# Two early loads moved from SyncE's queue to ScalarE's, in a fused linear-attention and cosine-gated MLP kernel

## The chip, the cores and the metric

The kernel runs on one core of a Trainium2 chip. A core has TensorE (PE: matrix products, written to PSUM), VectorE (DVE), ScalarE (ACT: functions such as exp, ln, sin), GpSimd (POOL) and SyncE (SP, which here issues DMA transfers), each with its own instruction stream, tied together by semaphores. The metric is device time in microseconds for one execution of the whole program.

## The reference

For each of 4 x 8 heads, a state of 48 x 48 is decayed and added to at each of 768 tokens; the result for all heads goes through a two-layer MLP with the gate h * cos(h).

```python
f = 1.0 / (1.0 + np.exp(-f_logit))
for t in range(S):                       # S = 768, D = 48
    state = f[:, :, t, :, None] * state + np.einsum('bhd,bhe->bhde', k[:, :, t], v[:, :, t])
    y[:, :, t] = np.einsum('bhd,bhde->bhe', q[:, :, t], state)
x = y.transpose(0, 2, 1, 3).reshape(3072, 384)
h = x @ w_in                             # 384 x 2048
out = (h * np.cos(h)) @ w_out            # 2048 x 384
```

q, k, v and f_logit are float32 of shape (4, 8, 768, 48), the output is float32 of shape (3072, 384).

## The kernel before, in words

The recurrence is computed in chunks. A chunk has 128 tokens; the work unit of the first half is a pair of chunks (256 tokens, all 8 heads), and there are 12 pairs, three for each batch entry. A pair n needs its parts of f, k, q and v, of shape 128 partitions x 8 heads x 2 tokens x 48. For the pairs 0 and 1 (`HALVES`) f, k and q are loaded and processed in two halves of four heads each, named `.0` and `.1`: `f0.1` is the second half of f for pair 0. Each half is 192 KB.

The steps for one half u of pair n, in the order in which they depend on each other:

- `f`, `q`, `k`: the three loads (line 299, function `load`).
- `ex`, `ln` (ACT, lines 332 and 336): exp(-f_logit), then ln(1 + ...), which gives the negative log of the gate.
- `fx` (ACT, line 350): the gate of the odd tokens, exp of the negative logarithm. It needs `ln`.
- `cum` (PE, lines 377 and 383): running sums of the logarithms, by a product with a triangular matrix.
- `eb`, `ei` (ACT, line 394 for the pairs in halves): the decay factors exp(-sum) and exp(+sum).
- `qa` (DVE, line 341) and `ka` (line 354): q and k of one token of each two are multiplied in place; `qa` needs f after `ex` and the loaded q, `ka` needs `fx` and the loaded k.
- `qm`, `km` (line 407): q and k times their decay factors, as bf16.
- `tq`, `tk` (PE, line 437), `qkt` (line 200): transposes and their copy out of PSUM.
- `sc`, `am` (lines 459 and 465 or 471), `ps`, `st`, `sz` (lines 489, 507, 513), `y`, `yi`, `xe` (line 541 and 200): scores, state and output of the pair.

The MLP takes the 3072 tokens in units of 128 or 256: `h` (line 608, first product), `co` (line 613, sine with a quarter turn), `g` (line 580, gate), `o` (line 630, second product), `ot` and `out`.

Nothing is planned at run time or by a scheduler: the string `ORDER` lists every step as `name:engine and buffers`, with the letters T (PE), S (ACT), V (DVE), G (POOL) and Y (SP). `emit` walks this list and emits each step's instructions on the engine that the letter names, so each engine's program is the list cut to its letter. The words that count here are, in the order of the list, with other engines left out:

```
SP before:   f0.1 f0.0 q0.0 k0.1 f1.1 k0.0 q0.1 q1.1 f1.0 k1.1 v0 q1.0 k1.0 f2 v1 w0.0 ...
ACT before:  (table load) ex0.1 ln0.1 ex0.0 ln0.0 fx0.0 eb0.0 ei0.0 eb0.1 ei0.1 fx0.1 ex1.1 ln1.1 fx1.1 ...
DVE before:  (constants, zeros) qa0.0 qm0.0 ka0.1 km0.1 ka0.0 km0.0 qa0.1 qa1.1 qm0.1 zvt.0 qm1.1 qkt0.1 ...
```

All loads are on SP's queue. In each engine's program an instruction waits for what it needs and holds back what stands behind it. In gaps of the beginning PE multiplies zeros (`zf0` to `zf46`, line 267, results never read).

[...] Steps that need exp or ln carry `table="E"`, the sine `table="S"`. `emit` starts with `table = None`, so the first step with "E", `ex0.1`, is preceded by a table load (line 673); line 673 also gives the loads at later changes from "S" to "E".

Of the kernel before, what the change touches and what calls it, by code (L numbers as in the profile page):

```python
# [15 lines left out]
B, H, S, D = 4, 8, 768, 48  # L16
# [20 lines left out]


ORDER = """
zsp.1:V zqk.1:V zqk.2:V zsz.0:G f0.1:Y0 ex0.1:S ln0.1:S1 f0.0:Y ex0.0:S ln0.0:S fx0.0:S zf0:T6  # L40
zf1:T6 zf2:T6 zf3:T6 zf4:T6 zf5:T6 zf6:T6 zf7:T6 cum0.1:T0 zf8:T6 cum0.0:T1 zsz.3:V eb0.0:S0
q0.0:Y0 ei0.0:S0 eb0.1:S ei0.1:S fx0.1:S qa0.0:V k0.1:Y0 qm0.0:V2 ka0.1:V zqk.0:G f1.1:Y1 km0.1:V
ex1.1:S zf9:T6 zf10:T6 zf11:T6 zf12:T6 zf13:T6 zf14:T6 zf15:T6 tq0.0:T2 ln1.1:S1 zf16:T6 zf17:T6
zf18:T6 zf19:T6 zf20:T6 tk0.1:T3 cum1.1:T0 k0.0:Y ka0.0:V km0.0:V zf21:T6 tk0.0:T fx1.1:S q0.1:Y
qa0.1:V q1.1:Y1 qa1.1:V ei1.1:S1 eb1.1:S1 qm0.1:V zvt.0:V qm1.1:V0 qkt0.0:S0 zf22:T6 zf23:T6 zf24:T6
# [146 lines left out]
def describe(nc, cpool, ppool, q, k, v, f_logit, moe_w_in, moe_w_out, out):  # L192
    G = Graph()
    eng = lambda e: {"DVE": nc.vector, "POOL": nc.gpsimd, "ACT": nc.scalar, "SP": nc.sync}[e]
# [63 lines left out]
    tiles = [ppool.tile([128, 1024], F32, name=f"ps_{i}") for i in range(4)]  # L258
# [37 lines left out]

    def load(name, val, src, b, c, h0, h1):
        tok = src[b, h0:h1, 2 * C * c:2 * C * c + 2 * C, :] if nc is not None else None
        G.step(name, ("SP",), lambda e: eng(e).dma_start(  # L299
            out=val.ap.rearrange("p h e d -> p h (e d)"),  # L300
            in_=tok.rearrange("h (p e) d -> p h (e d)", e=2)), writes=[val])

    def fetch(kind, pool, src, n, b, c, cut):

        whole = Val(pool)
        hs = [whole.part(lambda a, u=u: a[:, 4 * u:4 * u + 4]) for u in range(2)]
        if cut:
            for u in range(2):
                load(f"{kind}{n}.{u}", hs[u], src, b, c, 4 * u, 4 * u + 4)
        else:  # L310
            load(f"{kind}{n}", whole, src, b, c, 0, H)
        return whole, hs
# [343 lines left out]
def emit(tc, G, tiles):  # L656
    nc = tc.nc
    plan = []
    for word in ORDER.split():
        name, how = word.split(":")  # L660
        plan.append((G.steps[name], LETTER[how[0]], [int(x) for x in how[1:].split(",") if x]))
    assert len(plan) == len(G.steps)
    table, users = None, [[] for _ in tiles]
    for s, e, places in plan:
        for w in s.writes:
            v = w.whole
            if v.pool is not None and v.slot is None:
                v.slot = places.pop(0)
            w.first, w.final = not w.begun, w.left == 1
            w.begun, w.left = True, w.left - 1  # L670
        if s.table is not None:
            if s.table == "E" and table != "E":
                nc.scalar.preload_act_table_set("natural_log_exp_and_others")
            table = s.table
        n0 = nc.next_id()
        s.fn(e)
        made = (nc.find_inst_by_name(f"I-{i}") for i in range(n0 + 1, nc.next_id()))
        apart(tc, users, s, e, [i for i in made if i is not None])


def apart(tc, users, s, e, made):


    vals = [v.whole for v in s.reads + s.writes]
    banks = {b for v in vals if isinstance(v.pool, Banks) for b in range(v.slot, v.slot + v.pool.size)}
    home = lambda v: v.whole.pool is not None and not isinstance(v.whole.pool, Banks)
    uses = [(v, v.whole, i) for i, vs in enumerate((s.reads, s.writes)) for v in vs if home(v)]

    def meet(theirs):
        for v, w, wr in uses:  # L690
            for v2, w2, wr2 in theirs:
                if (wr or wr2) and w.pool is w2.pool and w.slot == w2.slot:
                    if w is not w2 or v is v2 or v is w or v2 is w2:
                        return True
        return False
    for t in {b // 2 for b in banks}:
        for engine, others, theirs, there in users[t]:
            if engine != e and not banks & theirs and not meet(there):
                for b in others:
                    for a in made:  # L700
                        tc.declare_no_dep(a, b, reason="the steps use different PSUM banks")
        users[t].append((e, made, banks, uses))
        del users[t][:-WITHIN]


@with_exitstack
def kernel(
    ctx: ExitStack,
    tc: tile.TileContext,
    q: bass.AP,  # L710
    k: bass.AP,
    v: bass.AP,
    f_logit: bass.AP,
    moe_w_in: bass.AP,
    moe_w_out: bass.AP,
    out: bass.AP,
):
    nc = tc.nc
    cpool = ctx.enter_context(tc.tile_pool(name="const", bufs=1))
    ppool = ctx.enter_context(tc.tile_pool(name="psum", bufs=1, space=bass.MemoryType.PSUM))  # L720
    with tc.manual_schedule():
        G, tiles = describe(nc, cpool, ppool, q, k, v, f_logit, moe_w_in, moe_w_out, out)
        emit(tc, G, tiles)
# [30 lines left out]
```

## Time and profile before

| what | value |
|---|---|
| median of 3 runs | 181.56 us (181.17 to 181.99) |
| profiled execution, its own time | 181.48 us |
| its span on the core | 179.4 us |
| busy: PE, DVE, ACT, POOL | 96%, 79%, 75%, 56% of the span |
| granted TensorE clock | full |
| first load issued, first function on ACT | 0.73 us, 3.49 us |
| queue of SP | 71968 packets, 33.37 MB |
| queue of ACT | 288 packets, 0.20 MB (two stores at the end) |

The span runs from the first instruction to the last one; the execution's time has 2.08 us more. In the rows of the profile a first number is a time from the start of the span in us and the second a length; `<-DMA q` in brackets names what ended the wait ahead of an instruction, with the idle time. `SPq` and `ACTq` are the sequencers of SP and ACT, which issue DMA transfers and take up waits; a row `DMA_DIRECT2D` is the issuing of a transfer, and "to landing" is the time from that issue to the semaphore that tells of the last byte. `PE busy (x)` and the like in rows of windows are busy time and number of instructions of PE, PEld (weight loads), DVE, ACT and POOL, then the granted clock, the busy share of the 16 DMA engines, and GB/s.

### The profile page before, as it was taken

The numbers are of one execution on the slowest core, as the hardware profiler recorded it, in microseconds if no ns is written. First come the engines' busy times: TensorE is split into PE (matmuls) and PEld (weight loads), VectorE is DVE, ScalarE is ACT, GpSimd is POOL, SyncE is SP. The second block draws the span as 40 slices with busy tenths as digits, with TensorE's granted clock in tenths as the row PEclk, the third lists the DMA queues.
The fourth block names the chain that finished last, engine by engine and source line by source line (L and its number), as shares of the span: only waits on it lengthen the run. The fifth ranks groups of instructions, "written<-read, shape, count | busy, mean of one in ns | idle before, by whom it ended". The sixth has DMA issues, their size and how long they took to land.

```text
span 179.4 us, 6015 instructions
## 1 busy us (share of the span) xinstructions
PE 172.6 (96%) x2553; PEld 125.2 (70%) x2553; DVE 142.5 (79%) x221; ACT 133.7 (75%) x190; POOL 100.5 (56%) x125
## 2 busy tenths in 40 slices
PE   7999999999999899999999999999999989999993
PEld 2565589867777588865588866888666668887662
DVE  6599999997598999979698896989768858874321
ACT  5969998988999998897689995877762478754020
POOL 4046559665979899989988959996061000000000
PEclk9999999999999999999999999999999999999999
DMA  5999999999999999789989999965308102000033
GB/s 125 278 262 306 371 331 355 324 286 277 243 263 283 252 272 218 160 161 257 270 203 219 253 212 263 192 107 117 91 4 211 41 17 74 4 0 0 26 114 127
DMA packets 72282, 33.94 MB, mean 189 GB/s; under 512 B 65344, under 2 KB 70720, under 8 KB 72256
## 3 DMA queue, kind: packets, MB, share of 16 engines
q1 hardware_dynamic: 71968, 33.37, 75.3%
q8 instruction: 20, 0.33, 0.8%
q10 hardware_dynamic: 288, 0.20, 0.3%
q14 instruction: 6, 0.05, 0.1%
HBM read 25.17 MB, written 4.72 MB: 167 GB/s over the span
## 4 chain that ended last, share of the span: by engine, by line
PE 75%; DVE 12%; DMA 5%; issue 3%; SPq 2%; ACT 1%; DVEq 0%; ACTq 0%
PE ps L608 35%; PE ps L630 29%; PE ps L541 4%; DVE sz L513 3%; PE ps L459 3%; DMA q<-in_q_dram 3%; SPq L299 2%; DMA out_dram<-ot 2%; PE ps L489 2%; DVE ps L507 2%; DVE am L471 2%; DVE am L465 1%; DVE ot L200 1%; PE ps L437 1%; DVE qkt L200 1%
## 5 line engine op out<-in xcount | busy, mean ns | idle before, releaser
L630 PE MATMUL ps<-w_out_bf,g 128*128 128x384 bf16 (+1 forms) x400 | 68.8, 320 | 0.0
L580 DVE TENSOR_TENSOR g<-ps,co 128x1024 bf16<-128x1024 f32 x48 | 60.8, 1307 | 9.2 <-ACT co L613 9.1
L608 PE MATMUL ps<-x,w_in_bf 128*128 128x256 bf16 (+1 forms) x624 | 66.2, 264 | 0.3 <-DVE g L580 0.2
L608 PEld LDWEIGHTS <-w_in_bf 128*128 128x128 bf16 x624 | 56.6, 98 | 8.4 <-DVE x L200 0.3
L613 ACT ACTIVATE co<-ps,halfpi 128x1024 bf16<-128x1024 f32 x48 | 51.9, 1113 | 10.7 <-PE ps L608 10.6
L630 PEld LDWEIGHTS <-g 128*128 128x128 bf16 x400 | 36.8, 98 | 20.4
L471 DVE TENSOR_TENSOR am<-ps,pmask 128x1024 bf16<-128x1024 f32 x22 | 26.2, 1215 | 2.4 <-PE ps L459 2.2
L407 POOL TENSOR_TENSOR qk<-k,bi 128x384 bf16<-128x384 f32 x20 | 19.9, 1001 | 9.8 <-ACT bi L398 9.3
L407 POOL TENSOR_TENSOR qk<-q,b 128x384 bf16<-128x384 f32 x20 | 20.1, 1005 | 2.9 <-ACT b L398 1.2
L354 POOL TENSOR_TENSOR k<-k,f 128x384 f32<-128x384 f32 (+1 forms) x11 | 10.6, 967 | 11.9 <-DMA k<-in_k_dram 9.6
L513 DVE TENSOR_TENSOR sz<-ps,b 64x192 bf16<-64x192 f32 x40 | 14.1, 352 | 2.6 <-PE ps L489 1.6
L200 ACT COPY ot<-ps 128x384 f32<-128x384 f32 (+1 forms) x14 | 6.1, 451 | 12.7 <-PE ps L630 12.7
L267 PE MATMUL ps<-zero 128*128 128x512 bf16 x47 | 14.4, 427 | 1.2 <-DVE zero L206 1.2
L200 DVE COPY ot<-ps 128x384 f32<-128x384 f32 (+1 forms) x12 | 6.4, 534 | 11.2 <-PE ps L630 9.7
L200 POOL COPY vt<-vb 64x384 bf16<-64x384 bf16 x27 | 13.4, 502 | 2.5 <-ACT vb L200 1.3
L507 DVE TENSOR_TENSOR ps<-ps,sz 64x192 f32<-64x192 f32 x32 | 11.7, 366 | 2.5 <-PE ps L489 1.5
L332 ACT ACTIVATE f<-f 128x768 f32<-128x768 f32 (+1 forms) x14 | 10.5, 751 | 3.8 <-DMA f<-in_f_logit_dram 3.7
L200 ACT COPY vt<-vb 64x384 bf16<-64x384 bf16 x21 | 10.7, 509 | 0.4
L366 POOL TENSOR_TENSOR sp<-ls 128x384 bf16<-128x384 f32 x10 | 10.0, 999 | 1.7 <-ACT ls L336 1.4
L200 DVE CAST x<-ps 128x384 bf16<-128x384 f32 x16 | 8.5, 552 | 1.6 <-PE ps L541 1.5
L200 ACT CAST x<-ps 128x384 bf16<-128x384 f32 x8 | 3.9, 483 | 7.9 <-PE ps L541 7.9
L613 ACT ACT_TABLE_LOAD x6 | 7.7, 1283 | 2.7 <-PE ps L608 2.6
(65 smaller groups left out, 177.8 us busy)
## 6 DMA issues: line engine op xcount, KB each, us to landing
v<-in_v_dram SPq DMA_DIRECT2D x12, 384.0 KB, 5.6
out_dram<-ot SPq DMA_DIRECT2D x22, 192.0 KB, 2.9
f<-in_f_logit_dram SPq DMA_DIRECT2D x10, 384.0 KB, 5.4
q<-in_q_dram SPq DMA_DIRECT2D x10, 384.0 KB, 6.2
k<-in_k_dram SPq DMA_DIRECT2D x10, 384.0 KB, 7.0
g<-in_moe_w_in_dram SPq DMA_DIRECT2D x4, 768.0 KB, 9.0
g<-in_moe_w_out_dram SPq DMA_DIRECT2D x4, 768.0 KB, 8.4
f<-in_f_logit_dram SPq DMA_DIRECT2D x4, 192.0 KB, 3.8
```

The costliest lines, as they stand in the source:

```text
L200: (nc.scalar.copy if e == "ACT" else eng(e).tensor_copy)(out=o, in_=i)
L267: G.step(f"zf{i}", ("PE",), lambda e, dump=dump: nc.tensor.matmul(dump.ap, lhsT=zero[:, 0:128], rhs=zero, start=True, stop=True), writes=[ ...
L332: nc.scalar.activation(out=flat(t.ap), in_=flat(t.ap), func=AF.Exp, scale=-1.0)
L354: eng(e).tensor_mul(out=w.ap[:, :, 0, :], in0=w.ap[:, :, 0, :], in1=t.ap[:, :, 0, :])
L407: G.step(f"{nm}{n}.{u}", ("POOL", "DVE"), lambda e, u=u, j=j, src=src, dec=dec: eng(e).tensor_mul(out=qkp[u][j].ap[:, :, :, 0:D], in0=swap ...
L471: G.step(f"am{n}.{u}", ("DVE",), lambda e, u=u, sc=sc: nc.vector.tensor_mul(out=am[u].ap.rearrange("p r b n -> p (r b) n"), in0=sc.ap.rear ...
L507: nc.vector.tensor_add(out=view()[s], in0=view()[s], in1=S0.ap[s, :, r, :])
L513: eng(e).tensor_mul(out=new.ap[s, :, r, :].rearrange("p (u a) n -> p u a n", u=2), in0=view()[s].rearrange("p (u a) n -> p u a n", u=2), i ...
L580: nc.vector.tensor_mul(out=o.rearrange("p b (n e) -> p b e n", e=2), in0=ph.ap.rearrange("p (b e n) -> p b e n", e=2, n=64), in1=co.ap.rea ...
L608: nc.tensor.matmul(ph.ap[:, i * T:(i + 1) * T].rearrange("p (g t) -> p g t", t=C), lhsT=w_in_bf[:, kk, f0:f0 + 128], rhs=xa[:, :, kk, :], ...
L613: G.step(f"co{m}.{j}", ("ACT",), lambda e, ph=ph, co=co: nc.scalar.activation(out=co.ap, in_=ph.ap, func=AF.Sin, bias=halfpi), reads=[ph], ...
L630: nc.tensor.matmul(po.ap[:, 0:c1 - c0], lhsT=gap[:, j, i * C:(i + 1) * C], rhs=w_out_bf[:, j, c0:c1], start=(po.first and j == 4 * s), sto ...
```

## The change

The loads `q0.0` and `k0.1` go from SP to ACT. In the list they now stand right behind `f0.1` and `f0.0` and ahead of `ex0.1`, and `f0.0` stands ahead of `ex0.1` and `ln0.1`; SP's program keeps its order without the two. The function `load` names ACT as an engine that may issue, and `emit` now starts with the table set "E" loaded explicitly ahead of the whole list, so that ACT's program begins with the table load, then issues `q0.0` and `k0.1`, then goes on with `ex0.1` as before. No other step moves on any engine.

```diff
 ORDER = """
-zsp.1:V zqk.1:V zqk.2:V zsz.0:G f0.1:Y0 ex0.1:S ln0.1:S1 f0.0:Y ex0.0:S ln0.0:S fx0.0:S zf0:T6
+zsp.1:V zqk.1:V zqk.2:V zsz.0:G f0.1:Y0 f0.0:Y q0.0:S0 k0.1:S0 ex0.1:S ln0.1:S1 ex0.0:S ln0.0:S fx0.0:S zf0:T6
 zf1:T6 zf2:T6 zf3:T6 zf4:T6 zf5:T6 zf6:T6 zf7:T6 cum0.1:T0 zf8:T6 cum0.0:T1 zsz.3:V eb0.0:S0
-q0.0:Y0 ei0.0:S0 eb0.1:S ei0.1:S fx0.1:S qa0.0:V k0.1:Y0 qm0.0:V2 ka0.1:V zqk.0:G f1.1:Y1 km0.1:V
+ei0.0:S0 eb0.1:S ei0.1:S fx0.1:S qa0.0:V qm0.0:V2 ka0.1:V zqk.0:G f1.1:Y1 km0.1:V
...
     def load(name, val, src, b, c, h0, h1):
         tok = src[b, h0:h1, 2 * C * c:2 * C * c + 2 * C, :] if nc is not None else None
-        G.step(name, ("SP",), lambda e: eng(e).dma_start(
+        G.step(name, ("SP", "ACT"), lambda e: eng(e).dma_start(
             out=val.ap.rearrange("p h e d -> p h (e d)"),
             in_=tok.rearrange("h (p e) d -> p h (e d)", e=2)), writes=[val])
...
-    table, users = None, [[] for _ in tiles]
+    table, users = "E", [[] for _ in tiles]
+    nc.scalar.preload_act_table_set("natural_log_exp_and_others")
```

## The prediction, made before the changed kernel ran

> **What bounds the kernel now.** I read the page first, then the chain of waits in its first 30 us, then the order of time of ScalarE (ACT) and VectorE (DVE) in that stretch, and then when each early load lands. The page's chain, by engine:
>
> ```profile
> span 179.4 us, 6015 instructions
> PE 75%; DVE 12%; DMA 5%; issue 3%; SPq 2%; ACT 1%; DVEq 0%; ACTq 0%
> ```
>
> The profiled execution took 181.48 us, its span 179.4, so 2.08 us lie around the span. My sum is made against 181.48; the median of the three runs is 181.56, 0.08 more. TensorE holds three quarters of the chain, but not its beginning. The chain in order of time (start, length, what):
>
> ```profile
> 1.25 0.49 SPq L299
> ...
> 5.04 4.51 DMA q<-in_q_dram
> ...
> 9.68 0.36 DVE q L341
> ...
> 22.76 0.48 DVE x L200
> ...
> 23.28 6.74 PE ps L608 x83
> ```
>
> Up to 5.04 us the chain is SyncE (SP) issuing loads one after another (the row shown is its second); then one transfer, the half q1.1 of the second pair, lands at 5.04 + 4.51 = 9.55; then DVE works to 23.24, and TensorE goes on from 23.28. What is lost or won before 23.28 is handed to TensorE, so I count it to the end one for one.
>
> Read at its face, this chain says that an SP issue fewer ahead of q1.1 is time won. DVE in order of time says how much:
>
> ```profile
> 5.93 0.36 DVE L341 SCALAR_TENSOR_TENSOR q<-f,q 128x192 f32<-128x192 f32 x1 [1.29 <-DMA q<-in_q_dram]
> 6.43 0.56 DVE L407 TENSOR_TENSOR qk<-q,b 128x384 bf16<-128x384 f32 x1
> 7.34 0.36 DVE L354 TENSOR_TENSOR k<-k,f 128x192 f32<-128x192 f32 x1 [0.35 <-ACT f L350]
> 9.07 0.35 DVE L341 SCALAR_TENSOR_TENSOR q<-f,q 128x192 f32<-128x192 f32 x1
> 9.68 0.36 DVE L341 SCALAR_TENSOR_TENSOR q<-f,q 128x192 f32<-128x192 f32 x1 [0.25 <-DMA q<-in_q_dram]
> ```
>
> The wait for q1.1 is 0.25 us. Before it DVE works without a pause from 7.34 to 9.42, and it could begin at 7.34 because ACT had finished the gate fx0.1. So behind the chain shown lies a second one, only 0.25 us shorter, and it runs through ACT:
>
> ```profile
> 0.73 1.28 ACT L673 ACT_TABLE_LOAD   x1 [0.73 <-PEq L738]
> 3.49 0.52 ACT L332 ACTIVATE f<-f 128x384 f32<-128x384 f32 x1 [1.47 <-DMA f<-in_f_logit_dram]
> 4.04 0.52 ACT L336 ACTIVATE sp<-f 128x384 bf16<-128x384 f32 x1
> 4.50 0.52 ACT L332 ACTIVATE f<-f 128x384 f32<-128x384 f32 x1
> 6.93 0.38 ACT L350 ACTIVATE f<-sp 128x192 f32<-128x192 bf16 x1
> ```
>
> ACT starts when the first f half (f0.1) lands, takes ex0.0 at 4.50, and ends fx0.1 at 7.31. Now the landings: issue times in the first fence (f0.0 is the 1.25 of the chain), and time from issue to landing in the second, in the order f0.1, f0.0, q0.0, k0.1.
>
> ```profile
> 0.73 1.00 SPq L299 DMA_DIRECT2D f<-in_f_logit_dram  x2
> 1.79 0.50 SPq L299 DMA_DIRECT2D q<-in_q_dram  x1
> 2.33 0.51 SPq L299 DMA_DIRECT2D k<-in_k_dram  x1
> ```
>
> ```profile
> f<-in_f_logit_dram SPq DMA_DIRECT2D x1, 192.0 KB, 2.7
> ...
> f<-in_f_logit_dram SPq DMA_DIRECT2D x1, 192.0 KB, 3.2
> ...
> q<-in_q_dram SPq DMA_DIRECT2D x1, 192.0 KB, 4.0
> ...
> k<-in_k_dram SPq DMA_DIRECT2D x1, 192.0 KB, 4.2
> ```
>
> They land at 0.73 + 2.7 = 3.43, 1.25 + 3.2 = 4.45, 1.79 + 4.0 = 5.79 and 2.33 + 4.2 = 6.53 us. The second f half, f0.0, lands 0.05 us before ACT takes it at 4.50: it has **no slack**, and fx0.1, DVE's step at 7.34 and all after it hang on it. From the fourth landing (6.53) to the eighth (q1.1, 9.55) there are four loads in 3.02 us, 0.755 each, while SP issues one in about 0.55 (1.79 to 2.33). So the loads queue in the DMA engines and not at SP: 196.6 kB in 0.755 us is 260 GB/s.
>
> **The change, part by part.**
>
> *SP's side.* Two issues go, and all later ones on SP come about 2 x 0.54 = 1.1 us earlier (1.79 to 2.33 to 2.88 by the rows' spacing), q1.1's too. It does not land 1.1 us earlier: before it the same eight halves have to move, six through SP's queue and two through ACT's, and the eighth landing stays near 9.55. Even if it came early, DVE gains at most its 0.25 us of waiting; then fx0.1 holds it. Gain taken: 0, bounds 0 and -0.25.
>
> [...]
>
> *ACT's side.* q0.0 and k0.1 stand on ACT behind the table load and ahead of ex0.1. Two issues at about 0.5 us (SP's rows) are done by 1.8 us at the earliest start, or by 3.1 if they wait for the load's end at 2.01. ACT waits for f0.1 until 3.49 either way, so the issues cost ACT nothing; without that cover they would cost 1.0 us. The table load is the first instruction of ACT before and after, so naming it ahead of the plan costs nothing.
>
> When do they go out? Two places show ACT's sequencer ahead of its engine:
>
> ```profile
> 51.17 1.28 ACT L673 ACT_TABLE_LOAD   x1
> ```
>
> ```profile
> L398 ACTq EVENT_SEMAPHORE  x1: 1002/1002/1002, 51.7 to 51.7; - x1
> ```
>
> ```profile
> 170.93 0.92 ACT L200 COPY ot<-ps 128x384 f32<-128x384 f32 x3 [5.07 <-PE ps L630]
> 171.66 0.34 ACTq L642 DMA_DIRECT2D out_dram<-ot  x1
> ```
>
> A wait is taken up at 51.7, 0.5 us into a table load that ends at 52.45; and a DMA is issued at 171.66 while the three copies ahead of it run to 171.85. So I expect q0.0 to be issued during the first table load, some 0.1 to 0.5 us after SP's f0.1, and k0.1 about 0.5 us later.
>
> *The price.* Then q0.0 and k0.1 travel **beside f0.1 and f0.0** and no longer behind them. What the DMA engines moved (the last two columns are their busy share and GB/s):
>
> ```profile
> 1.00:2.00 1.00, 0.81 (x2) 0.28 (x3) 0.51 (x8) 1.00 (x1) 0.92 (x4) 1.00 0.07 18
> 2.00:3.00 1.00, 1.00 (x4) 0.43 (x3) 0.93 (x5) 0.02 (x1) 0.63 (x2) 1.00 0.94 224
> 3.00:4.00 1.00, 1.00 (x4) 0.33 (x3) 0.88 (x7) 0.51 (x1) 0.00 (x0) 1.00 0.93 236
> 4.00:5.00 1.00, 1.00 (x7) 0.52 (x6) 0.64 (x3) 0.97 (x3) 0.00 (x0) 1.00 0.96 227
> 5.00:6.00 1.00, 1.00 (x13) 0.52 (x12) 0.07 (x1) 0.90 (x3) 0.00 (x0) 1.00 1.13 309
> ```
>
> By these rows the engines are 0.93 to 0.96 busy, so a second stream is paid by the first. f0.1's 196.6 kB have moved at 2 + (196.6 - 18) / 224 = 2.80, and it lands at 3.43: 0.63 us from moved to landed. How late f0.0 comes, no row of before shows, since there one queue is at work; the bounds:
> - nothing, if the second queue only takes what is free;
> - three halves moved when f0.0 is through (q0.0 half served): 705 - 227 = 478 kB by 4.0, the missing 112 at 227 GB/s, so 4.49 + 0.63 = 5.12, 0.67 us late;
> - four halves, in equal shares: 705 kB by 5.0, the missing 81 at 309, so 5.26 + 0.63 = 5.89, 1.44 us late;
> - four halves, taken by the fourth landing of before: 6.53, 2.08 us late.
>
> I take equal shares less the head start: ACT's stream begins some 0.4 us behind SP's, 0.4 x 115 = 46 kB at half the rate, about 0.2 us. So f0.0 is **1.2 us late**, at about 5.65 (nearest to the third bound, as its rates are those of this very stretch). f0.1 shares too and comes perhaps 0.5 us later; that is hidden, since ex0.1 and ln0.1 then still end before f0.0 lands.
>
> What is queued behind ex0.0 on ACT: ln0.0, fx0.0, the four exponentials of the decays, fx0.1, then ex1.1. TensorE waits for ln0.0 with its sums, DVE for the decays (its step at 6.43) and for fx0.1. All move by 1.2. DVE takes k0.1 at 7.34 + 1.2 = 8.54, comes to q1.1 at 9.42 + 1.2 = 10.62, finds it landed (9.55), and the old wait of 0.25 is gone. q0.0 and k0.1 come early enough: DVE needs them at 5.93 + 1.2 at the latest and at 8.54.
>
> **Sum:** +1.2 - 0.25 = +0.95 us at 23.28 us, none of it covered later. 181.48 + 0.95 = 182.4 us. Beside the median that is +0.5%, just about what a measurement of this kernel can tell from no change (0.5%, 0.9 us).
>
> **The rivals.**
>
> 1. *ACT's issues wait for the end of the table load* (2.01). f0.1 goes from its issue at 0.73 to the first bytes just before 2.0, 1.2 us, so the second stream starts at 3.2. Then 18 + 224 + 47 = 289 kB have moved, 104 kB of f0.0 are missing, and at half of 236 they take 0.88 us in place of 0.44: 0.44 late, less 0.25 is +0.2, **181.7 us**. For it: the load is the instruction ahead. Against it: the rows at 51.7 and 171.66. From a first issue on ACT later than about 2.0 on, this decides.
>
> 2. *The second queue fills what the first leaves* (the other side). In 2 to 5 us the engines move 224 to 236 GB/s, and 309 in the next row. If two queues reach 309 at once, 80 GB/s x 3 us = 240 kB go through on top; f0.0 lands at 4.45 as before, q1.1 240 / 260 = 0.9 us sooner, and DVE's 0.25 is won: **181.2 us**. It decides if f0.0 lands by 4.50. Against it: a busy share of 0.93 to 0.96.
>
> 3. *The chain at its face*: SP's two issues count in full, -1.1 us, **180.4 us**. For it: the chain of waits. Against it: 7.31, where ACT frees DVE; only with f0.0 earlier could DVE begin earlier, and SP's first two issues stay where they are.
>
> 4. *Equal shares at the slow rate*, f0.0 as late as the fourth landing of before: 2.08 - 0.25 = +1.83, **183.3 us**. For it: these are real landings; against it: they hold the tail of a queue that had by then run on into the fifth load.
>
> [...]
>
> **How the numbers follow.** My forecast (ACT's stream beside both f halves, f0.0 0.67 to 1.9 us late) 0.64, own range 181.9 to 183.1; rival 1 0.15; rival 2 0.08; rival 3 0.05; rival 4 0.08. Slower by over 0.5% (over 182.47): a little over half of my case, 0.35, and rival 4, together 0.43. Faster by over 0.5%: rival 3 and 0.03 of unknowns, 0.08. Within: the rest, 0.49. The range that should hold 8 in 10 goes from 181.1 (rival 2) to 183.3 (rival 4).
>
> **What would show it.** In the changed kernel's trace: ACT's first load issue before 2.0 us (right) or after (rival 1); f0.0 landing, and with it the second exponential on ACT, at about 5.65 in place of 4.50 (4.50: rival 2); the first DVE step that waits for fx0.1 at about 8.5 in place of 7.34; no wait for q at DVE's fourth q step; the first TensorE work of line 608's long run at about 24.2 in place of 23.28. SP's issues 1.1 us earlier with landings still 0.75 apart would show that the queue at SP was not the bound. I am wrong if the second exponential keeps its time, or if it is late and TensorE's long run is not.

## The result, and the profile after

The changed kernel is **slower by 2.5%**: median 185.98 us of four executions (185.9 to 186.8) against 181.59 us of four of the kernel before (181.17 to 181.99), ratio 1.0252 with a 95% interval of 1.0215 to 1.0289. That is +4.4 us where +0.95 was forecast, and beyond the upper end of the range, 183.3. The profiled execution took 185.93 us with a span of 183.8, so 2.1 us lie around the span as before, and the 4.4 us are inside it. In some of the kernels further down a part of the executions takes some 3 us longer; their ratios are made from the others, and experiments 12 to 14 look at them.

The chain of waits of the changed kernel (start, length, what), in its beginning and at two later places:

```profile
1.25 4.54 DMA f<-in_f_logit_dram
5.81 0.53 ACT f L332
...
8.66 0.37 DVE k L354
...
10.39 0.62 DVE q L341 x2
11.01 0.88 DVE qk L407
...
25.21 0.33 PE ps L608 x3
25.54 1.80 issue
27.34 9.94 PE ps L608 x129
37.27 0.89 PE ps L437 x16
...
88.35 4.39 DMA out_dram<-ot
```

The chain no longer begins with SP's issues and q1.1: it begins with f0.0, which lands at 1.25 + 4.54 = 5.79 us. The two later places in the chain of the kernel before:

```profile
33.40 0.89 PE ps L437 x16
...
84.52 3.79 DMA out_dram<-ot
```

With 23.28, the start of the long run of line 608 before, this divides the loss:

| place | before | after | later by | added in this stretch |
|---|---|---|---|---|
| first k product on DVE | 7.34 | 8.66 | 1.32 | 1.32 |
| end of the last q product | 10.04 | 11.01 | 0.97 | -0.35 |
| long run of line 608 begins | 23.28 | 25.20 | 1.92 | 0.95 |
| first transposes behind it (line 437) | 33.40 | 37.27 | 3.87 | 1.95 |
| a store of the middle ends (84.52 + 3.79; 88.35 + 4.39) | 88.31 | 92.74 | 4.43 | 0.56 |

Up to the second line it goes as the prediction had it: 0.97 where 0.95 was forecast. Three more amounts come behind it: 0.95, 1.95 and 0.56. From the store on the two kernels run alike.

ACT in order of time, the changed kernel, answers to ACT's rows of before:

```profile
0.73 1.28 ACT L664 ACT_TABLE_LOAD   x1 [0.73 <-PEq L739]
0.76 0.49 ACTq L299 DMA_DIRECT2D q<-in_q_dram  x1
1.28 0.56 ACTq L299 DMA_DIRECT2D k<-in_k_dram  x1
4.26 0.52 ACT L332 ACTIVATE f<-f 128x384 f32<-128x384 f32 x1 [2.25 <-DMA f<-in_f_logit_dram]
...
5.81 0.52 ACT L332 ACTIVATE f<-f 128x384 f32<-128x384 f32 x1 [0.47 <-DMA f<-in_f_logit_dram]
```

Both issues go out during the table load, and each leaves within 0.03 us of one of SP's (0.74 and 1.25). The second exponential starts at 5.81, not at 4.50. The two loads of a pair share: f0.1 lands at 4.24 in place of 3.46 and q0.0 at 4.63, f0.0 at 5.79 and k0.1 at 6.12, so within a pair the landings lie 0.39 and 0.33 us apart, where those of one queue lie 0.75 apart.

**The 0.95.** DVE and POOL in order of time, the changed kernel:

```profile
10.93 0.95 DVE L407 TENSOR_TENSOR qk<-q,b 128x384 bf16<-128x384 f32 x1
...
12.08 1.08 DVE L407 TENSOR_TENSOR qk<-q,b 128x384 bf16<-128x384 f32 x1
13.08 0.68 DVE L200 COPY qkt<-ps 128x1024 bf16<-128x1024 bf16 x1
```

```profile
10.79 0.68 POOL L354 TENSOR_TENSOR k<-k,f 128x192 f32<-128x192 f32 x1 [8.15 <-DMA k<-in_k_dram]
11.54 1.20 POOL L407 TENSOR_TENSOR qk<-k,bi 128x384 bf16<-128x384 f32 x1
```

and the kernel before:

```profile
9.95 0.55 DVE L407 TENSOR_TENSOR qk<-q,b 128x384 bf16<-128x384 f32 x1
...
10.69 0.49 DVE L407 TENSOR_TENSOR qk<-q,b 128x384 bf16<-128x384 f32 x1
11.13 0.69 DVE L200 COPY qkt<-ps 128x1024 bf16<-128x1024 bf16 x1
```

```profile
11.16 0.59 POOL L354 TENSOR_TENSOR k<-k,f 128x192 f32<-128x192 f32 x1 [8.52 <-DMA k<-in_k_dram]
11.83 1.00 POOL L407 TENSOR_TENSOR qk<-k,bi 128x384 bf16<-128x384 f32 x1
```

Before, POOL took up the loaded half k1.1 at 11.16, just as DVE ended its two products of q (10.69 + 0.49 = 11.18). Now the products come 0.98 later and POOL 0.37 earlier, because SP's later loads land earlier. They overlap: the products take 0.95 and 1.08 us in place of 0.55 and 0.49, together 0.99 more, and POOL's product 1.20 in place of 1.00. Experiment 7 says how much of the 0.95 this is.

**The 1.95.** After three products of the long run TensorE stands for 1.80 us, and what ended the wait is only "issue": no engine and no load. In that time one transfer of another kind is at work. Transfers by queue, in two short windows in which it starts, 24.85 to 24.95 us after and 20.9 to 21.0 before (queue and kind: packets, MB, share of 16 engines):

```profile
q8 instruction: 1, 0.02, 69.5%
```

```profile
q8 instruction: 1, 0.02, 61.8%
```

The page of the changed kernel counts 20 such packets with 0.33 MB (16384 bytes each in the single records), and 2549 + 2553 recorded products and weight loads on TensorE, 255 for each packet. So I take them for TensorE's own program; that a packet brings 256 instructions is my estimate from these counts. Start and end of the second packet, in us, and how long it starts after TensorE's 512th recorded instruction, worked out from the single records:

| kernel | starts | that long after the 512th | ends | long run begins | goes on after the stop |
|---|---|---|---|---|---|
| before | 20.96 | 2.07 | 21.95 | 23.28 | no stop |
| after | 24.88 | 4.04 | 25.99 | 25.20 | 27.34 |

After, TensorE goes on 1.35 us after the packet's end. By the same 1.35 the packet of the kernel before was good from 23.30, and the instruction at which the changed kernel stops, three products into the long run, came at 23.45: on this reading the old kernel had about 0.15 us of slack there, and no row of it shows a stop. The lateness is there at the first packet already: it starts at 13.93 before, 0.16 after TensorE's 256th recorded instruction, and at 18.10 after, 2.55 behind it.

### The profile page after: what moved, and what is told of

Read it like the earlier page. It is cut to its first block, busy times and chain, and to the rows that moved or that the text cites. A ratio compares the mean times of both kernels' runs of the same rounds, so it can differ in the third digit from the quotient of the medians.

```text
span 183.8 us, 6011 instructions
## 1 busy us (share of the span) xinstructions
PE 172.2 (94%) x2549; PEld 125.0 (68%) x2553; DVE 143.2 (78%) x221; ACT 133.5 (73%) x190; POOL 101.3 (55%) x125
## 4 chain that ended last, share of the span: by engine, by line
PE 74%; DVE 8%; ACT 7%; DMA 5%; issue 4%; SPq 0%; DVEq 0%; ACTq 0%
PE ps L608 34%; PE ps L630 28%; PE ps L541 4%; PE ps L459 3%; DMA f<-in_f_logit_dram 2%; DMA out_dram<-ot 2%; PE ps L489 2%; ACT vt L200 2%; DVE sz L513 2%; PE ps L437 1%; DVE qk L407 1%; DVE ps L507 1%; PE ps L377 1%; DVE ot L200 1%; ACT f L332 1%
## 5 line engine op out<-in xcount | busy, mean ns | idle before, releaser
L267 PE MATMUL ps<-zero 128*128 128x512 bf16 x43 | 13.1, 426 | 1.5 <-DVE zero L206 1.2
```

The source lines that it names most:

```text
L267: G.step(f"zf{i}", ("PE",), lambda e, dump=dump: nc.tensor.matmul(dump.ap, lhsT=zero[:, 0:128], rhs=zero, start=True, stop=True), writes=[ ...
```

## The experiments

Fourteen more runs were made, one of them of the kernel before. All kernels compute the whole result; where zero products are taken out, these are ones whose results nobody reads. The order of words is given as a diff of the list, and the expectations name the theories by letters.

**1 to 3: what is it about the two loads?** The first keeps all loads on SP and only makes f0.0 the third load, as late as the change made it, with nothing on ACT's queue. The second moves k0.1 alone. The third gives ACT its loads behind the first exponential, so that SP's stream goes first.

```diff
 sp_f_third (from the kernel before)
-f0.1:Y0 ex0.1:S ln0.1:S1 f0.0:Y ex0.0:S ... eb0.0:S0 q0.0:Y0 ei0.0:S0 ...
+f0.1:Y0 q0.0:Y0 ex0.1:S ln0.1:S1 f0.0:Y ex0.0:S ... eb0.0:S0 ei0.0:S0
 only_k_on_act (from the kernel after)
-f0.0:Y q0.0:S0 k0.1:S0 ex0.1:S ... eb0.0:S0 ei0.0:S0
+f0.0:Y k0.1:S0 ex0.1:S ... eb0.0:S0 q0.0:Y0 ei0.0:S0
 act_behind_ex (from the kernel after)
-f0.0:Y q0.0:S0 k0.1:S0 ex0.1:S ln0.1:S1
+f0.0:Y ex0.1:S q0.0:S0 k0.1:S0 ln0.1:S1
```

> Kernel before with only one thing changed: on SyncE's queue q0.0 is issued between f0.1 and f0.0, so that f0.0 is the third load and not the second; nothing is on ScalarE's queue. Theory A (all of the 4.4 us starts from the late second half of f, whatever the queue): f0.0 lands near 5.79 as the third landing of the kernel before, the second exponential starts near 5.8, the first k product of VectorE near 8.6, TensorE's long run stops again, and the total is 3.5 to 4.6 us above the kernel before. Theory B (the second queue costs by itself, in the fetching of TensorE's instructions for one): the second exponential is as late, but the long run does not stop, and the total is 1.0 to 2.2 us above.

> Changed kernel with q0.0 back on SyncE at its old place (third); only k0.1 is issued by ScalarE. One half travels beside the f halves in place of two. Theory A (lateness of f0.0 is the cause): f0.0 lands between the 4.47 of the kernel before and the 5.79 of the changed one, near 5.1 to 5.3, VectorE's first k product is 0.6 to 0.8 us later than before, and the total is 0.4 to 0.6 us above the kernel before if TensorE's long run does not stop, 2 to 3 if it does. Theory B (a load on the second queue costs by itself): 3 us or more above.

> Changed kernel with the two issues put behind the first exponential in ScalarE's program. That exponential waits until f0.1 lands. If ScalarE's sequencer goes on past an instruction that waits, the loads are issued near 0.8 and 1.3 us as in the changed kernel and the total is the same, 4.4 us above the kernel before. If it holds, they are issued near 3.5, f0.0 lands near 4.5, q0.0 near 6.6 and k0.1 near 7.5, the first k product of VectorE starts between 7.4 and 7.8, and by theory A the total is within 0.7 us of the kernel before.

sp_f_third: ratio 1.0060 (1.0025 to 1.0094), +1.1 us. DVE, then TensorE, in order of time:

```profile
8.55 0.36 DVE L354 TENSOR_TENSOR k<-k,f 128x192 f32<-128x192 f32 x1 [0.36 <-ACT f L350]
...
10.81 0.55 DVE L407 TENSOR_TENSOR qk<-q,b 128x384 bf16<-128x384 f32 x1
...
11.56 0.67 DVE L407 TENSOR_TENSOR qk<-q,b 128x384 bf16<-128x384 f32 x1
```

```profile
24.49 6.73 PE L608 MATMUL ps<-x,w_in_bf 128*128 128x128 bf16 x83
```

f0.0 is nearly as late as in the changed kernel (first k product 8.55 against 8.66), the long run begins 1.21 late, and TensorE has no stop in it. The idea that the lateness of f0.0 alone carries the 4.4 us falls: by itself it costs about 1.1 (three of the ten executions, at 185.9 to 187.5, are not in this ratio).

only_k_on_act: ratio 1.0038 (1.0013 to 1.0063). f0.0 lands at 5.18, the long run begins at 23.99, 0.71 late, and a small stop follows. So one of the two loads alone costs 0.7 of the 4.4 us (in eight of ten executions; two took 185.3 and 185.6); q0.0 alone was not tried. TensorE in order of time:

```profile
23.99 0.34 PE L608 MATMUL ps<-x,w_in_bf 128*128 128x128 bf16 x3
24.91 6.28 PE L608 MATMUL ps<-x,w_in_bf 128*128 128x128 bf16 x75 [0.57 <-issue]
```

act_behind_ex: 187.64 us, ratio 1.0318 (1.0259 to 1.0376), the slowest of all, where theory A had expected at most 0.7 us more than before. ACT, then DVE, then TensorE, in order of time:

```profile
3.58 0.52 ACT L332 ACTIVATE f<-f 128x384 f32<-128x384 f32 x1 [1.56 <-DMA f<-in_f_logit_dram]
3.58 0.44 ACTq L299 DMA_DIRECT2D q<-in_q_dram  x1
4.05 0.54 ACTq L299 DMA_DIRECT2D k<-in_k_dram  x1
```

```profile
8.97 0.36 DVE L341 SCALAR_TENSOR_TENSOR q<-f,q 128x192 f32<-128x192 f32 x1 [4.32 <-ACT sp L336]
```

```profile
29.18 5.07 PE L608 MATMUL ps<-x,w_in_bf 128*128 128x128 bf16 x61 [1.66 <-issue]
```

Here the issues do wait, behind an exponential that waits for f0.1. The two loads then take, from issue to landing (transfers in a short window at the two issues):

```profile
q<-in_q_dram ACTq DMA_DIRECT2D x1, 192.0 KB, 5.2
...
k<-in_k_dram ACTq DMA_DIRECT2D x1, 192.0 KB, 6.0
```

So q0.0 lands at 8.8 and k0.1 at 10.0, behind the six loads that SP had issued before them; the last of these, q1.1, lands at 8.36. (f0.0 is early here, at 4.20.) With the prediction's 1.2 us to the first bytes, 0.63 from moved to landed and 0.755 for each half, equal shares would have q0.0 land after two halves, at 3.58 + 1.2 + 1.51 + 0.63 = 6.9, and k0.1 after four, at 8.4. In this run, then, loads issued at 3.43 (SP), 3.58 and 4.05 us (ACT) landed in the order of issue, at 8.36, 8.8 and 10.0; those of the changed kernel, issued within 0.03 us of each other, shared, with landings 0.39 and 0.33 apart. DVE then waits for q0.0; the releaser that the row names had long been done.

**4: is the stop the end of the fetched instructions?** The changed kernel without the zero products zf9 to zf32, 24 products and their 24 weight loads that stand ahead of the long run. If the stop is where the fetched program ends, it has to move by 24 pairs.

```diff
-... zf9:T6 zf10:T6 ... zf31:T4 zf32:T4 ...
```

> Changed kernel without 24 of the 47 products of zeros (zf9 to zf32), whose results nobody reads, so TensorE has 48 instructions less before its long run of line 608. Theory C (the 1.8 us stop at 25.5 us is TensorE running out of fetched instructions: the packet of 16 KB that brings the next ones started at 24.88, 4 us after TensorE's 512th instruction): the stop moves behind 24 more pairs of instructions of the long run, about 2.6 us of work, and shrinks or goes; the total is 1.2 to 2.2 us below the changed kernel. Rival D (the stop is a wait for data, say for weights): it stays at the same place in the program, and the total is within 0.5 us of the changed kernel. If the granted clock falls without the zeros, all products are slower and the total says nothing.

186.08 us, ratio 1.0214 (1.0170 to 1.0258). TensorE in order of time:

```profile
26.27 1.68 PE L609 MATMUL ps<-x,w_in_bf 128*128 128x128 bf16 x27
28.87 5.33 PE L609 MATMUL ps<-x,w_in_bf 128*128 128x128 bf16 x58 [0.93 <-issue]
```

The stop comes after 27 products in place of three: 24 later, to the pair. That it is the end of the fetched instructions is shown by this. The other traces agree: nine have such a stop in the long run, of 0.41 to 1.80 us, and each time 698 or 702 instructions of TensorE are recorded ahead of it (some traces lack four records); TensorE goes on 1.27 to 1.48 us after the packet's end. The total did not get better, since the long run itself began at 26.27 and not 25.20, and the packet was later too (26.15). This is the case that the expectation had set aside: without the zero products TensorE's products were slow up to some 20.7 us (three of those left take 1.46 us at 17.90, four take 1.03 at 20.93).

**5 and 6: why is the packet late?** It starts 2.07 us after TensorE's 512th instruction before and 4.04 after. Either loads on ACT's queue hold it up, or it waits behind the loads of the weights (w0.0 to w0.2, which SP issues from 12 us on) because it is asked for later than before. The first of the two kernels has nothing on ACT's queue, but the weight load w0.0 early; the second is the changed kernel with the load q2 ahead of the weights.

```diff
 sp_third_w_first (from sp_f_third)
-k1.0:Y ... f2:Y0 ... v1:Y1 w0.0:Y0
+k1.0:Y w0.0:Y0 ... f2:Y0 ... v1:Y1
 after_q2_first (from the kernel after)
-v1:Y1 w0.0:Y0 ... w0.1:Y1 ... q2:Y0
+v1:Y1 q2:Y0 w0.0:Y0 ... w0.1:Y1 ...
```

> The kernel with f0.0 as SyncE's third load (nothing on ScalarE's queue), and with the first part of the weights, w0.0, issued ahead of f2 and v1 on SyncE, so that its rows of 2 KB are under way when TensorE asks for more instructions. Theory E (the packet of TensorE's instructions waits behind weight rows that stand in the queue ahead of it; the changed kernel only brings the two together): the first such packet, which started at 15.45 in the kernel with f0.0 third, starts at 16.5 or later, the second one (21.82) later too or at least not earlier, TensorE's long run stops, and the total is 0.7 to 2 us above that kernel. Theory B (what delays the packet is the use of ScalarE's queue): both packets start as in the kernel with f0.0 third, no stop, and the total is within 0.5 us of it.

> Changed kernel with q2 issued ahead of the weights w0.0 to w0.2 on SyncE, so that the rows of 2 KB set in about 1.5 us later. Theory E: the first packet of instructions, at 18.10 in the changed kernel, starts between 15.6 and 17; the second one, at 24.88, starts earlier by 0.5 us or more, and the stop of 1.8 us in TensorE's long run shrinks by as much; the total is 0.5 to 1.8 us below the changed kernel, unless a weight that now lands later holds the long run up. Theory B: the packets start as in the changed kernel and the total is within 0.4 us of it.

sp_third_w_first: 183.95 us, ratio 1.0105 (1.0056 to 1.0154, from three of four executions; the fourth took 186.2). TensorE in order of time:

```profile
24.48 0.34 PE L608 MATMUL ps<-x,w_in_bf 128*128 128x128 bf16 x3
26.53 4.64 PE L608 MATMUL ps<-x,w_in_bf 128*128 128x128 bf16 x57 [1.71 <-issue]
```

The long run begins where that of sp_f_third did (24.49), and then it stops for 1.71 us, as long as in the changed kernel, with nothing on ACT's queue. The packet starts at 24.04 (sp_f_third: 21.82). So ACT's queue isn't needed for the stop; an earlier weight load is enough. after_q2_first: 184.45 us, ratio 1.0170 (1.0117 to 1.0224), 1.5 us less than the changed kernel, with executions from 183.4 to 185.7. In the profiled one, the shortest, the packet starts at 23.51 and the stop is 0.58:

```profile
25.96 8.27 PE L608 MATMUL ps<-x,w_in_bf 128*128 128x128 bf16 x102 [0.58 <-issue]
```

**7: does POOL lengthen DVE's products?** The changed kernel with the loads k1.1 and v0 exchanged, so that POOL has its half later.

```diff
-f1.0:Y ... k1.1:Y1 ... v0:Y0
+f1.0:Y ... v0:Y0 ... k1.1:Y1
```

> Changed kernel with k1.1 and v0 exchanged on SyncE, so that k1.1 lands 1.5 us later, near 12.1, and GpSimd starts its products of k1.1 after VectorE's two products of q (0.95 and 1.08 us long in the changed kernel, 0.55 and 0.49 in the kernel before). Theory F (the two products are slow because GpSimd works at the same time): they take 0.5 to 0.6 us again, and VectorE reaches its score masks 0.6 to 0.9 us earlier. By theory C (TensorE runs out of instructions) the long run still cannot go on before 1.35 us after its second packet of instructions has landed (25.99 in the changed kernel), so that most of this is not seen in the total: 0 to 0.7 us below the changed kernel. Rival: the products stay slow, as their data is late or the slowness comes from the transfers; same total.

Ratio 1.0081 (1.0044 to 1.0117) from five executions of 182.4 to 183.9 us; the other five took 185.4 to 186.4, about as long as the changed kernel. DVE in order of time:

```profile
10.94 0.55 DVE L407 TENSOR_TENSOR qk<-q,b 128x384 bf16<-128x384 f32 x1
...
11.68 0.49 DVE L407 TENSOR_TENSOR qk<-q,b 128x384 bf16<-128x384 f32 x1
12.46 0.69 DVE L200 COPY qkt<-ps 128x1024 bf16<-128x1024 bf16 x1 [0.28 <-PE ps L437]
```

The same products at the same time as in the changed kernel (10.93), and they take 0.55 and 0.49 again, as POOL now begins at 12.29. The overlap is shown as the cause of the slow products. Of the 0.99 won, 0.62 is left at the score masks (13.06 against 13.68 us) and 0.59 at the long run (24.61). The rest goes into a wait of DVE for TensorE's transposes, the last row: they come at 12.03, and 10.71 in the kernel before, as late as f0.0. So without the overlap the long run is 1.33 us late, as much as the first k product (8.67 against 7.34), and the wait of 0.25 that DVE was rid of is paid after all. sp_f_third says the same: 1.21 late at both places. The total of the five fell by more than expected, because the packet came earlier too (23.26) and the stop shrank to 0.97.

**8: was there time to be had in the old wait?** The kernel before, with a clearing step of DVE put into its wait of 0.25 us, and four late zero products left out.

```diff
-qa0.1:V q1.1:Y1 qa1.1:V ei1.1:S1 eb1.1:S1 qm0.1:V zvt.0:V qm1.1:V0 ... zf43:T6 zf44:T6 zf45:T6 zf46:T6
+qa0.1:V zvt.0:V q1.1:Y1 qa1.1:V ei1.1:S1 eb1.1:S1 qm0.1:V qm1.1:V0 ...
```

> Kernel before, all loads on SyncE, with VectorE's zeroing of a buffer (0.27 us) moved into its wait of 0.25 us for q1.1, and without the last four products of zeros, so that TensorE has 8 instructions less before it needs its second packet. If the start of the long run is VectorE's and the code allows it: 23.0 in place of 23.28, and 0.2 to 0.4 us less than the kernel before, about 181.3 to 181.6. If the packet of instructions (21.95 plus 1.35 us in the kernel before, 23.30) is the limit: nothing is gained.

Ratio 1.0002 (0.9973 to 1.0030): nothing. In the profiled execution, the slowest of the twelve (182.77 us), f0.0 landed at 4.64, TensorE had a stop of 0.41 in the long run, and what DVE had won it lost again in a wait for TensorE's transposes:

```profile
11.75 0.69 DVE L200 COPY qkt<-ps 128x1024 bf16<-128x1024 bf16 x1 [0.59 <-PE ps L437]
```

That this wait is what takes the gain in the other executions too is likely, but not shown.

**9 to 11: the two side effects taken back together.** after_both is the changed kernel with both exchanges (7 and 6). sp_third_q2_first and before_q2_first put q2 ahead of the weights in sp_f_third and in the kernel before.

```diff
 after_both: both diffs of 6 and 7
 sp_third_q2_first, before_q2_first:
-v1:Y1 w0.0:Y0 ... q2:Y0
+v1:Y1 q2:Y0 w0.0:Y0 ...
```

> Changed kernel with both cures: k1.1 behind v0 and q2 ahead of the weights on SyncE. Theory G (the 4.4 us are four pieces: f0.0 1.3 us late, VectorE's two products 0.7 slowed by GpSimd, TensorE's instructions late by 1.95, and about 0.5 in a store at 85 us that follows from these): only the first piece is left, the long run starts near 24.5 and does not stop or by less than 0.4 us, and the total is 0.9 to 1.5 us above the kernel before. Rival B (ScalarE's queue costs by itself): 2.5 us or more remain.

> Kernel with f0.0 as SyncE's third load, nothing on ScalarE's queue, and q2 ahead of the weights. With f0.0 third alone, some executions took 3 to 5 us more than the rest. Theory E (TensorE's packet of instructions against the weight rows, with next to no slack): with the weights 1.5 us later the executions lie together, 0.8 to 1.3 us above the kernel before. Rival: they scatter as before, so that something else makes the long ones.

> Kernel before with q2 ahead of the weights on SyncE. Theory E gives TensorE's second packet some 1 us of slack; in the kernel before it lands 1.35 us ahead of the moment at which it is needed (21.95 against 23.30) and the long run starts at 23.28, so the slack is worth nothing in an execution like the profiled one and up to 0.5 us in others: 181.4 to 182.0, against 181.9. If a weight lands too late for the first products of the MLP: 0.5 us or more slower.

after_both: 1.0061 (1.0032 to 1.0090) from five executions of 182.35 to 183.4; the other five took 185.2 to 185.9. sp_third_q2_first: 1.0054 (1.0029 to 1.0080), 182.4 to 184.1. before_q2_first: 1.0041 (1.0021 to 1.0061), a loss: a weight now comes late, and TensorE waits for POOL's cast of it shortly before the long run:

```profile
22.73 0.84 PE L608 MATMUL ps<-x,w_in_bf 128*128 128x128 bf16 x12 [0.85 <-POOL w_in_bf L200]
```

So the order q2 first is a remedy for the stop only; in the kernel before it costs about 0.4%.

**12 to 14: why do some executions take 3 us longer?** The profiled execution of after_both is one of the long ones. TensorE in its beginning, in order of time, and the row of a window that covers its zero products (the granted clock is the third number from the end):

```profile
5.39 0.33 PE L377 MATMUL ps<-sp,incl 128*128 128x192 bf16 x2 [0.89 <-ACT sp L336]
...
6.83 0.33 PE L377 MATMUL ps<-sp,incl 128*128 128x192 bf16 x2 [0.80 <-ACT sp L336]
...
7.10 2.77 PE L267 MATMUL ps<-zero 128*128 128x512 bf16 x7
```

```profile
7.10:9.30 2.20, 2.20 (x12) 0.86 (x10) 1.27 (x3) 2.07 (x8) 0.00 (x0) 0.60 1.28 261
```

Seven zero products take 2.77 us where the changed kernel has

```profile
7.21 1.67 PE L267 MATMUL ps<-zero 128*128 128x512 bf16 x7
```

and the granted clock is down to 0.60 in the window (0.50 from 7.52 to 10.93 us). The long run begins at 26.18 and stops for 0.67 us. The late halves of f have made TensorE wait for ACT's logarithms twice, 0.89 and 0.80 us; the kernel before was busy there. Two kernels put zero products into these waits: after_both_warm is after_both with three ahead of each of the two sums, sp_third_warm is sp_f_third with three ahead of the second. before_again is the kernel before once more.

```diff
 after_both_warm (from after_both)
-zf7:T6 cum0.1:T0 zf8:T6 cum0.0:T1 ... zf9:T6 zf10:T6 zf11:T6 zf12:T6 zf13:T6 zf14:T6
+zf7:T6 zf9:T6 zf10:T6 zf11:T6 cum0.1:T0 zf8:T6 zf12:T6 zf13:T6 zf14:T6 cum0.0:T1 ...
 sp_third_warm (from sp_f_third)
-zf8:T6 cum0.0:T1 ... zf9:T6 zf10:T6 zf11:T6
+zf8:T6 zf9:T6 zf10:T6 zf11:T6 cum0.0:T1 ...
```

> The kernel before once more, with a profile from the chip of these runs. All theories: no load on ScalarE's queue, f0.0 landing at 4.4 to 4.7, TensorE's second packet of instructions starting between 20.5 and 22.3 us, and its long run at 23.2 to 23.9.

> Changed kernel with both cures, and with six of the products of zeros moved into the stretches in which TensorE waits for the late halves of f (three ahead of cum0.1, three ahead of cum0.0); nothing added. Theory H (after these idle stretches TensorE's products run at half speed for a while in some executions, and this makes the long ones of 185 to 186 us): the executions lie together between 182.3 and 183.8. Rival B (ScalarE's queue costs by itself in some executions): as before about half of them are at 185 to 186.

> Kernel with f0.0 as SyncE's third load and three products of zeros moved into the stretch of 1.15 us in which TensorE waits for f0.0. Theory H: no executions of 185 us or more, where the same kernel without the move had three of ten; the rest at 182.2 to 183.5 as before. Rival: long ones remain.

before_again: 181.18 us, f0.0 at 4.15 (earlier than expected), second packet at 20.64, long run at 23.24. after_both_warm: 1.0055 (1.0026 to 1.0084), all ten executions from 182.1 to 183.9. TensorE in order of time:

```profile
6.71 0.33 PE L377 MATMUL ps<-sp,incl 128*128 128x192 bf16 x2 [0.18 <-ACT sp L336]
...
24.20 8.99 PE L608 MATMUL ps<-x,w_in_bf 128*128 128x128 bf16 x112
```

sp_third_warm: 1.0030 (1.0004 to 1.0056), all ten from 182.05 to 182.95, where sp_f_third had three of ten at 185.9 to 187.5. With the waits filled the long executions are gone in both. That the half-speed stretch is what makes them long is not shown: only one of them was profiled, and sp_third_q2_first speaks against it. None of its ten executions took more than 184.1 us, though nothing fills the wait there, and its profiled execution has the slow stretch behind a wait of 1.51 us (the clock column stays at 1.00 there, but the products take as long):

```profile
7.58 2.84 PE L267 MATMUL ps<-zero 128*128 128x512 bf16 x7
```

Its long run begins at 26.16, as in after_both, but without a stop, and the execution took 184.06 us. So the slow stretch alone doesn't make an execution long; that it does so together with a late packet would fit, and stays open. The long run of after_both_warm begins at 24.20, with ACT's loads in place and no stop. That the prediction had put it at 24.2 is in part luck: f0.0 landed at 5.56 here, and with zero products moved ahead TensorE's transposes were no longer as late. No version here beats the kernel before.

## Why the prediction was wrong, step by step

1. **What bounds the kernel: right.** The chain of q1.1 stood only 0.25 us ahead of a second chain through f0.0 and ACT, and f0.0 had no slack. The changed kernel's chain begins with f0.0.
2. **SP's side gives nothing: right for DVE, incomplete otherwise.** From the single records, the fifth to the eighth landing are at 6.87, 7.62, 8.38 and 9.13 us, 0.75 apart as forecast, but some 0.42 earlier than before (7.31 to 9.55), where I had the eighth stay at 9.55. I costed this only for DVE, which could win nothing by it. What it set going was POOL: k1.1's steps began at 10.79 in place of 11.16.
3. **ACT's issues cost ACT nothing and go out beside the table load: right.** 0.76 and 1.28 us, in the forecast stretch. Rival 1 (they wait for the load's end) is out. In act_behind_ex they were held to 3.58, not by a table load but by an exponential with an open wait.
4. **f0.0 is 1.2 us late: right in size, but equal shares hold only in part.** It landed at 5.79 for 5.65; the second exponential moved by 1.31. 5.79 is also where the third landing of before lay (1.79 + 4.0), and SP's f0.0 was the third of the four issues by time. The two readings give nearly the same time here. That two queues share equally was my assumption, and no run shows it as a rule: act_behind_ex speaks for order of issue where loads are issued 0.15 us or more apart (3.43, 3.58 and 4.05 us, landed at 8.36, 8.8 and 10.0); within the two pairs of the changed kernel the loads did share, which made f0.1 0.78 late where I had put 0.5, with landings 0.39 and 0.33 apart. Where the order arises no run here tells. Rivals 2 and 3 needed f0.0 by 4.50 and fall.
5. **+1.2 - 0.25: right on DVE, but the second term was not to be had.** +1.32 at the first k product, the two q steps back to back without a wait (10.39, two in 0.62), +0.97 at their end. But TensorE was as late as DVE. Where POOL hardly disturbs DVE, in after_k11_late and sp_f_third, the long run is late by 1.33 and 1.21, as much as the first k product; in the first of them DVE waits 0.28 for the transposes where it had waited 0.25 for q1.1. sp_f_third has the lateness with no load on ACT, and it costs +1.1 us in all.
6. **"+0.95 us at 23.28 us, none of it covered later", handed to TensorE one for one: this step failed**, three times.
   - Between DVE's q steps and 23.28 it grew by 0.95: 0.59 by the overlap with POOL (experiment 7), and 0.36 that would have been lost without it, as the 0.25 came back (step 5). The old order had POOL begin 0.02 us before DVE's end, and I moved DVE later without asking what runs beside its new place. The lengthened steps are shown (0.95 and 1.08 us for DVE's products, 1.20 for POOL's, against 0.55, 0.49 and 1.00 in the kernel before and in after_k11_late); by what the two hold each other up, the rows don't tell.
   - At 25.54 TensorE ran out of instructions: 1.95 us. I treated TensorE from 23.28 on as bound by work. The chain of before had no row for the fetch, as by my estimate above it had arrived 0.15 us in time. Experiment 4 shows what the stop is, experiment 5 that with a weight load issued earlier the packet comes late without ACT's queue (24.04 in place of 21.82). In after TensorE came to its 512th recorded instruction 1.95 us later (20.84 against 18.89), and I take it that the packet was asked for later by as much; that this alone makes the extra 1.97 of delay is not shown, since I couldn't move the request without moving loads.
   - A store in the middle took 4.39 in place of 3.79: 0.56. I have not tested why.
7. **What would have shown me wrong.** The second exponential came within 0.16 us of its sign (5.81 for 5.65). The long run was off by 1.0 (25.20 for 24.2), which shows the first part of step 6 and the 0.25 of step 5. For the rest I had no sign: 2.51 of the 4.43 us lie behind the beginning of the long run, where I stopped looking.

Rival 4 (183.3) had the right sign, but its mechanism isn't what happened either: f0.0 came at 5.79, not 6.53.

## What to carry to other kernels

When a change makes one step late, list what runs beside its new place, not only what waits for it: here DVE's late products met POOL's early ones, and the moved loads made both happen. Look also at transfers of kind "instruction" ahead of a long run of short products: in the kernel before such a packet had by my estimate 0.15 us to spare and no row of waits showed it, and when it started 3.92 us later, TensorE stood for 1.80. And when a wait on one engine is about to go, look at what else its next step waits for: the 0.25 us that DVE no longer waited for q1.1 it would have waited for TensorE (0.28 in after_k11_late). Here the second queue for loads gave no second stream: from 7 to 23.3 us the transfers moved 309 GB/s, and 307 in the kernel before, and the loads put on it landed in order of issue (act_behind_ex) or within 0.4 us of the one issued beside them (the changed kernel). So the one to move forward is the one that the critical chain waits for.

## What the runs showed of the hardware that I had not expected

- TensorE stood still for its own program: stops of 1.80 (the changed kernel), 1.71 (sp_third_w_first), 1.66 (act_behind_ex), 0.93 (after_fewer_zeros) and 0.58 us (after_q2_first), each with "issue" as what ended it, and each time TensorE went on 1.27 to 1.48 us after the end of a packet of 16384 bytes. In the kernel before that packet ended at 21.95, and the long run from 23.28 on has no stop.
- After waits in its beginning TensorE's next products were slow in two profiles, after_both (waits of 0.89 and 0.80 us, granted clock 0.50 from 7.52 to 10.93) and sp_third_q2_first (a wait of 1.51, granted clock 1.00): seven products in 2.77 and 2.84 us, not 1.67. In the changed kernel waits of 0.60 and 0.91, and in sp_f_third one of 1.15, passed without it. What decided, no run here shows.
- Loads on two queues landed nearly in order of issue where they were issued 0.15 us or more apart: in act_behind_ex ACT's two, issued at 3.58 and 4.05 us, at 8.8 and 10.0, behind all six that SP had issued by 3.43, the last of which landed at 8.36. Issued within 0.03 us of each other, in the changed kernel, they shared: f0.1 landed at 4.24 in place of 3.46.
